# Attention start of a fused kernel: v loaded by unit, the mask and square read from PSUM, one transpose copy moved to ScalarE

## The chip, the cores and the metric

The kernel runs on one core of a Trainium2 chip. The metric is device time of one execution in microseconds, the median of three runs. Times inside the execution come from a profile of one run, counted from the first instruction.

## The reference

Two stages follow each other. The first is an attention with a squared ReLU in place of the softmax, for 8 batches, 12 heads, 448 tokens and a head size of 64. The second is a dense layer with the same activation, on all 3584 tokens.

```python
scores = q @ k.T / sqrt(64)                       # per batch and head, 448 x 448
attn   = max(scores, 0) ** 2 / 448
x      = attn @ v                                  # heads side by side: 3584 x 768
h      = x @ w_in                                  # 3584 x 2048
out    = max(h, 0) ** 2 @ w_out                    # 3584 x 768
```

## The kernel before: the parts concerned

Four heads make a unit, three units make a batch, and the 24 units are numbered n. A unit takes seven rounds, each with 64 keys of every head. A round has four steps: scores on TensorE into a PSUM tile (two such tiles exist), squared ReLU into a tile "at" of fp16, and, three rounds later, the product with v. The rounds are counted from 0 (r = 7n + t). TensorE's order is fixed by the program text; the orders of VectorE, ScalarE and GpSimd are set by the scheduler.

```python
s_p   = tile_pool(name="sps", bufs=2, space=PSUM)     # score tiles, two banks each
mm_p  = tile_pool(name="mmps", bufs=4, space=PSUM)
rel_p = tile_pool(name="widep", bufs=5)               # fp32 tiles in SBUF
at_p  = tile_pool(name="atp", bufs=14)

def load_v(b, parts):                                 # four loads for a batch, each with all three units
    ...
    for i in parts:
        r, e, h = ((0, 0, 0), (1, 0, 2), (0, 1, 3), (1, 1, 1))[i]
        nc.gpsimd.dma_start(out=vst[b][64 * r:64 * r + 64, :, e, :], in_=src[h])

def relu2(ps, dst, scale):                            # L148, L149
    nc.scalar.activation(out=dst, in_=ps, func=AF.Square, scale=scale)
    nc.vector.scalar_tensor_tensor(
        out=dst, in0=ps, scalar=0.0, in1=dst, op0=ALU.is_gt, op1=ALU.mult)

def relu2_wide(ps, dst, scale, eng):                  # L155, L156
    r = rel_p.tile([P, 2, S], FP32, name="rel", tag="wide")
    nc.scalar.activation(out=r, in_=ps, func=AF.Relu, scale=scale)
    eng.tensor_mul(dst, r, r)

def soft(n, t, sp):
    at = at_p.tile([P, 2, S], FP16, name="at", tag="at")
    if n < NPE:                                       # NPE = 6: the first 42 rounds
        relu2_wide(sp[:, :, 0:S], at, SK, nc.gpsimd if n and t == 4 else nc.vector)
    else:
        relu2(sp[:, :, 0:S], at, SK)

def turn_pe(n, w, op):                                # transposes of k and q for units 0 to 5
    ps = mm_p.tile([P, TJ * P], FP16, name="tps", tag="mm")
    for t in range(TJ):
        nc.tensor.transpose(ps[:, t * P:(t + 1) * P], src[:, t, :], ident)
    op(t.rearrange("p t c -> p (t c)"), ps)           # L103, the copy out of PSUM

# the first 23 rounds: attention alone
for r in range(STREAM):                               # STREAM = 23, LAG = 3
    sp = scores(n, t)
    soft(n, t, sp)
    for z in late.get(r, (r - LAG,) if LAG <= r else ()):
        av(*divmod(z, TJ))                            # TensorE: product with v of an earlier round
    ...                                               # loads, casts, transposes of later units

# then two rounds a step, the products with v of a whole unit in one burst,
# and a share of the queued dense matmuls (hps, later ops)
for i in range(STREAM // 2, NB):
    ...
```

From unit 6 on, k and q are transposed by DMA and `relu2` is used throughout.

Of the kernel before, what the change touches and what calls it, by code (L numbers as in the profile page):

```python
# [16 lines left out]
def kernel(  # L17
# [9 lines left out]
    nc = tc.nc  # L27

    B, H, S, D = q.shape
# [7 lines left out]
    TJ = S // TP  # L37
    NU = 3
# [5 lines left out]
    SK = 256.0  # L44
# [29 lines left out]
    def load_qk(n, w, eng):  # L74
        b, u = divmod(n, NU)
        t = raw_p.tile([P, 2, TJ * D], FP32, name=w + "f", tag=w + "f")
        src = q if w == "q" else k
        eng.dma_start(
            out=t,
            in_=src[b, 4 * u:4 * u + 4].rearrange(  # L80
                "(f e) (p t) d -> (e p) f (t d)", e=2, t=TJ))
        raw[n, w] = t

    def cast_qk(n, w, op):
        src = raw.pop((n, w))
        t = blk_p.tile([P, TJ, 2 * D], FP16, name=w + "s", tag=w + "s")
        op(t.rearrange("p t (f d) -> p f t d", f=2),  # L87
           src.rearrange("p f (t d) -> p f t d", d=D))
        blk[n, w] = t

    def turn_dma(n, w):
        t = qkt_p.tile([P, TJ, P], FP16, name=w + "T", tag=w + "T")
        nc.sync.dma_start_transpose(
            out=t, in_=blk.pop((n, w)).rearrange("p t c -> p (t c)"))
        qkt[n, w] = t

    def turn_pe(n, w, op):
        src = blk.pop((n, w))
# [3 lines that stand above are left out]
        t = qkt_p.tile([P, TJ, P], FP16, name=w + "T", tag=w + "T")  # L102
        op(t.rearrange("p t c -> p (t c)"), ps)  # L103
        qkt[n, w] = t

    def load_v(b, parts):
        if b not in vst:
            vst[b] = v_p.tile([P, NU, 2, TJ * D], FP16, name="vs", tag="vs")
        src = v[b].rearrange("(u x) (p t) d -> x p u (t d)", x=4, t=TJ)
        for i in parts:  # L110
            r, e, h = ((0, 0, 0), (1, 0, 2), (0, 1, 3), (1, 1, 1))[i]
            nc.gpsimd.dma_start(out=vst[b][64 * r:64 * r + 64, :, e, :], in_=src[h])  # L112

    w1 = [const_p.tile([P, NM, 512], FP16, name=f"w1_{i}", tag=f"w1_{i}") for i in range(4)]
    w2 = [const_p.tile([P, 4, DM], FP16, name=f"w2_{i}", tag=f"w2_{i}") for i in range(4)]
# [1 line left out]
    def load_w1(i):  # L117
        nc.gpsimd.dma_start(
            out=w1[i],
            in_=moe_w_in[:, 512 * i:512 * (i + 1)].rearrange("(m p) f -> p m f", p=P))  # L120

    def load_w2(i):
        nc.gpsimd.dma_start(
            out=w2[i],
            in_=moe_w_out[512 * i:512 * (i + 1), :].rearrange("(f p) d -> p f d", p=P))
# [21 lines left out]
    def relu2(ps, dst, scale):  # L147
        nc.scalar.activation(out=dst, in_=ps, func=AF.Square, scale=scale)  # L148
        nc.vector.scalar_tensor_tensor(  # L149
            out=dst, in0=ps, scalar=0.0, in1=dst, op0=ALU.is_gt, op1=ALU.mult)  # L150

    def relu2_wide(ps, dst, scale, eng):

        r = rel_p.tile([P, 2, S], FP32, name="rel", tag="wide")
        nc.scalar.activation(out=r, in_=ps, func=AF.Relu, scale=scale)  # L155
        eng.tensor_mul(dst, r, r)  # L156

    def h_groups(b):
        pr = b // 2
# [89 lines left out]

    def soft(n, t, sp):  # L250
        at = at_p.tile([P, 2, S], FP16, name="at", tag="at")
        if n < NPE:
            relu2_wide(sp[:, :, 0:S], at, SK, nc.gpsimd if n and t == 4 else nc.vector)
        else:
            relu2(sp[:, :, 0:S], at, SK)
        ats[n, t] = at
# [3 lines left out]
    def av(n, t):  # L260

        b, u = divmod(n, NU)
        if n == NU * b and t == 0:
            xts[b] = x_p.tile([P, NM, S], FP16, name="xt", tag="xt")
        vs = vst[b]
        if t == 0:
            avs_open[n] = [mm_p.tile([P, 512], FP32, name="avt", tag="mm") for _ in range(2)]
        ap = avs_open[n]
        at = ats.pop((n, t))
        for e in range(2):  # L270
            for c in range(2):
                f = c ^ e
                r = slice(64 * c, 64 * c + 64)
                nc.tensor.matmul(  # L274
                    ap[f][64 * e:64 * e + 64, 0:S],
                    lhsT=vs[r, u, e, t * D:(t + 1) * D],
                    rhs=at[r, e, :],
                    start=(t == 0), stop=(t == TJ - 1), skip_group_check=True)
        if t < TJ - 1:
            return  # L280
        for f in range(2):
            nc.scalar.activation(
                out=xts[b][:, 2 * u + f, :], in_=ap[f][:, 0:S], func=AF.Copy, scale=CX)

    pool, dve, act = nc.gpsimd.tensor_copy, nc.vector.tensor_copy, nc.scalar.copy
# [3 lines left out]
    NPE = 6  # L289
# [11 lines left out]
    def upkeep(i):  # L301

        for n in range(NU, NUN):
            b, u = divmod(n, NU)
            if i == max(TJ * n // 2, STREAM // 2):
                if 5 < n + 3 < NUN:
                    for w in "kq":
                        load_qk(n + 3, w, nc.sync)
                if n == 3:
                    for z in range(4):  # L310
                        load_w2(z)
                if u == 0 and b < B - 1:
                    load_v(b + 1, range(4))
            if i == (TJ * n + 4) // 2:
                if n + 2 < NUN:
                    for w in "kq":
                        cast_qk(n + 2, w, pool)
                if n + 1 < NPE:
                    for w in "kq":
                        turn_pe(n + 1, w, dve)  # L320
                if NPE <= n + 2 < NUN:
                    for w in "kq":
                        turn_dma(n + 2, w)

    with tc.manual_schedule():
        load_qk(0, "k", nc.sync)
        load_qk(0, "q", nc.scalar)
        for n in (1, 2):
            load_qk(n, "k", nc.sync)
            load_qk(n, "q", nc.sync)  # L330
        idle = const_p.tile([P, 512], FP16, name="idle", tag="idle")
        nc.vector.memset(idle, 0.0)
        ident = const_p.tile([P, P], FP16, name="ident", tag="ident")
        make_identity(nc, ident)
        load_v(0, range(4))

        warm = mm_p.tile([P, 512], FP32, name="warm", tag="mm")
        for _ in range(12):
            nc.tensor.matmul(warm, lhsT=idle[:, 0:P], rhs=idle, start=True, stop=True)
        cast_qk(0, "k", dve)  # L340
        cast_qk(0, "q", act)
        turn_pe(0, "k", dve)
        turn_pe(0, "q", dve)
        for w in "kq":
            cast_qk(1, w, pool)
        load_w1(0)

        beside = {
            1: [(load_w1, 1)],
            2: [(cast_qk, 2, "k", pool), (cast_qk, 2, "q", pool),  # L350
                (load_qk, 3, "k", nc.sync), (load_qk, 3, "q", nc.sync)],
            3: [(turn_pe, 1, "k", dve), (load_w1, 2)],
            5: [(turn_pe, 1, "q", dve), (load_w1, 3)],
            7: [(turn_pe, 2, "k", dve)],
            8: [(turn_pe, 2, "q", dve), (load_v, 1, (0, 1))],
            9: [(cast_qk, 3, "k", pool), (cast_qk, 3, "q", pool),
                (load_qk, 4, "k", nc.sync), (load_qk, 4, "q", nc.sync)],
            10: [(load_v, 1, (2, 3))],
            14: [(turn_pe, 3, "k", dve)],
            15: [(turn_pe, 3, "q", dve)],  # L360
            16: [(cast_qk, 4, "k", pool), (cast_qk, 4, "q", pool),
                 (load_qk, 5, "k", nc.sync), (load_qk, 5, "q", nc.sync)],
        }
        late = {21: (18, 19), 22: (20,)}
        for r in range(STREAM):
            n, t = divmod(r, TJ)
# [3 lines that stand above are left out]
                av(*divmod(z, TJ))  # L370
            for fn, *a in beside.get(r, ()):
                fn(*a)
# [3 lines left out]
    for i in range(STREAM // 2, NB):  # L376
        g = []
        for r in range(max(STREAM, 2 * i), 2 * i + 2):
            n, t = divmod(r, TJ)
            g.append((n, t, scores(n, t)))  # L380
        if i in avs:
            for t in range(TJ):
                av(avs[i], t)
        for a in g:
            soft(*a)
        if i in pushes:
            push_dense(pushes[i])
        upkeep(i)
        nxt = min([j for j in pushes if j > i] or [NB + 2])
        run_some(max(0.0, (queued - KEEP) / (nxt - i)))  # L390
# [40 lines left out]
```

## Time and profile before

| what | value |
|---|---|
| device time, median of three | 422.73 us |
| span in the profile | 419.6 us |
| TensorE busy | 395.6 us (94%) |
| VectorE busy | 259.2 us (62%) |
| ScalarE busy | 257.0 us (61%) |
| GpSimd busy | 85.8 us (20%) |
| L156, VectorE, at<-rel | 37 times, mean 1300 ns |
| L149, VectorE, at<-sp,at | 126 times, mean 1086 ns |
| L103, VectorE, kT and qT out of PSUM | 6 times each, 0.61 to 0.62 us |
| first product with v | starts at 10.22 us, its last matmul waits for v until 13.88 us |

The shares are means over the whole span; the kernel has a start of some 80 us, in which attention runs alone or with little dense work, and a long rest in which TensorE has dense work at all times. A row of groups names the line, the engine, the operation, what is written and read, the count, and the mean length of one.

### The profile page before, as it was taken

The numbers are of one execution on the slowest core, as the hardware profiler recorded it, in microseconds if no ns is written. First come the engines' busy times: TensorE is split into PE (matmuls) and PEld (weight loads), VectorE is DVE, ScalarE is ACT, GpSimd is POOL, SyncE is SP. The second block draws the span as 40 slices with busy tenths as digits, with TensorE's granted clock in tenths as the row PEclk, the third lists the DMA queues.
The fourth block names the chain that finished last, engine by engine and source line by source line (L and its number), as shares of the span: only waits on it lengthen the run. The fifth ranks groups of instructions, "written<-read, shape, count | busy, mean of one in ns | idle before, by whom it ended". The sixth has DMA issues, their size and how long they took to land.

```text
span 419.6 us, 7567 instructions
## 1 busy us (share of the span) xinstructions
PE 395.6 (94%) x3104; PEld 199.1 (47%) x3104; DVE 259.2 (62%) x305; ACT 257.0 (61%) x402; POOL 85.8 (20%) x97
## 2 busy tenths in 40 slices
PE   6677968899999999999999999999999999999995
PEld 2232433455455555454455555455455555555562
DVE  3899699885766566686767556677766653223100
ACT  4477869676767666777766565767766564333211
POOL 5973842610141010410141100311000000000000
PEclk9676999999999999999999999999999999999999
DMA  8999999794685643966474655957400111111132
GB/s 253 305 278 244 208 192 209 210 111 121 103 155 154 150 103 98 156 153 137 112 148 137 169 83 126 156 125 159 93 20 21 37 39 39 38 40 37 37 77 75
DMA packets 62883, 53.58 MB, mean 128 GB/s; under 512 B 35712, under 2 KB 59264, under 8 KB 62848
## 3 DMA queue, kind: packets, MB, share of 16 engines
q1 hardware_dynamic: 50672, 40.84, 41.1%
q0 software_dynamic: 11904, 11.80, 17.9%
q8 instruction: 24, 0.39, 0.4%
q10 hardware_dynamic: 272, 0.46, 0.3%
q14 instruction: 11, 0.09, 0.1%
HBM read 45.61 MB, written 11.01 MB: 135 GB/s over the span
## 4 chain that ended last, share of the span: by engine, by line
PE 85%; DVE 8%; DMA 2%; ACT 2%; issue 2%; POOL 1%; POOLq 0%; ACTq 0%
PE ops L198 35%; PE hps L170 34%; PE sp L244 8%; PE avt L274 7%; DVE at L156 6%; DMA vs<-in_v_dram 2%; ACT rel L155 1%; DVE qT L103 1%; POOL vs L112 0%; PE tps L101 0%; DVE kT L103 0%; DVE g L149 0%; DVE at L149 0%; ACT g L148 0%; ACT osb L205 0%
## 5 line engine op out<-in xcount | busy, mean ns | idle before, releaser
L149 DVE SCALAR_TENSOR_TENSOR at<-sp,at 128x896 f16<-128x896 f32 x126 | 131.6, 1086 | 66.0 <-ACT at L148 65.9
L148 ACT ACTIVATE at<-sp 128x896 f16<-128x896 f32 x126 | 108.8, 915 | 40.9 <-PE sp L244 40.5
L198 PEld LDWEIGHTS <-g 128*128 128x128 f16 x896 | 85.3, 98 | 66.6 <-issue 10.3
L149 DVE SCALAR_TENSOR_TENSOR g<-hps,g 128x448 f16<-128x448 f32 x128 | 77.6, 620 | 57.0 <-ACT g L148 56.3
L148 ACT ACTIVATE g<-hps 128x448 f16<-128x448 f32 x128 | 69.6, 550 | 36.0 <-PE hps L170 35.3
L205 ACT ACTIVATE osb<-ops 128x384 f32<-128x384 f32 x56 | 27.6, 494 | 59.5 <-PE ops L198 52.8
L87 POOL CAST ks<-kf 128x896 f16<-128x896 f32 x23 | 23.9, 1040 | 185.9 <-DMA kf<-in_k_dram 165.1
L244 PE MATMUL sp<-qT,kT 64*64 64x448 f16 x672 | 53.8, 376 | 6.6 <-DVE at L149 2.6
L274 PE MATMUL avt<-at,vs 64*64 64x448 f16 x672 | 43.7, 365 | 10.2 <-DVE at L156 3.6
L156 DVE TENSOR_TENSOR at<-rel 128x896 f16<-128x896 f32 x37 | 46.6, 1300 | 4.0 <-ACT rel L155 4.0
L198 PE MATMUL ops<-w_2_96,g 128*128 128x384 f16 x224 | 46.9, 326 | 0.0
L155 ACT ACTIVATE rel<-sp 128x896 f32<-128x896 f32 x42 | 36.9, 924 | 15.6 <-PE sp L244 13.1
L198 PE MATMUL ops<-w_0_94,g 128*128 128x384 f16 x224 | 46.4, 326 | 0.0
L198 PE MATMUL ops<-w_3_97,g 128*128 128x384 f16 x224 | 46.3, 326 | 0.0
L198 PE MATMUL ops<-w_1_95,g 128*128 128x384 f16 x224 | 46.1, 326 | 0.0
L170 PE MATMUL hps<-xt,w_1_91 128*128 128x448 f16 x192 | 41.0, 353 | 1.2 <-DVE g L149 1.2
L170 PE MATMUL hps<-xt,w_2_92 128*128 128x448 f16 x192 | 40.9, 353 | 0.0
L170 PE MATMUL hps<-xt,w_0_90 128*128 128x448 f16 x192 | 40.8, 359 | 0.0
L170 PE MATMUL hps<-xt,w_3_93 128*128 128x448 f16 x192 | 40.5, 353 | 0.0
L274 PEld LDWEIGHTS <-vs 64*64 64x64 f16 x672 | 22.4, 109 | 26.9 <-issue 13.3
L244 PEld LDWEIGHTS <-kT 64*64 64x64 f16 x672 | 15.0, 106 | 36.6 <-issue 32.3
L170 PEld LDWEIGHTS <-w_1_91 128*128 128x128 f16 x192 | 18.1, 98 | 20.0 <-issue 5.0
(33 smaller groups left out, 172.0 us busy)
## 6 DMA issues: line engine op xcount, KB each, us to landing
kf<-in_k_dram SPq DMA_DIRECT2D x24, 448.0 KB, 5.1
out_dram<-osb SPq DMA_DIRECT2D x56, 192.0 KB, 2.7
qf<-in_q_dram SPq DMA_DIRECT2D x23, 448.0 KB, 5.8
vs<-in_v_dram POOLq DMA_DIRECT2D x32, 168.0 KB, 5.2
w_0_90<-in_moe_w_in_dram POOLq DMA_DIRECT2D x1, 768.0 KB, 12.3
w_1_91<-in_moe_w_in_dram POOLq DMA_DIRECT2D x1, 768.0 KB, 20.2
w_2_92<-in_moe_w_in_dram POOLq DMA_DIRECT2D x1, 768.0 KB, 23.6
w_3_93<-in_moe_w_in_dram POOLq DMA_DIRECT2D x1, 768.0 KB, 26.9
```

The lines of the kernel that those rows point to most:

```text
L87: op(t.rearrange("p t (f d) -> p f t d", f=2), src.rearrange("p f (t d) -> p f t d", d=D))
L103: op(t.rearrange("p t c -> p (t c)"), ps)
L148: nc.scalar.activation(out=dst, in_=ps, func=AF.Square, scale=scale)
L149: nc.vector.scalar_tensor_tensor(out=dst, in0=ps, scalar=0.0, in1=dst, op0=ALU.is_gt, op1=ALU.mult)
L155: nc.scalar.activation(out=r, in_=ps, func=AF.Relu, scale=scale)
L156: eng.tensor_mul(dst, r, r)
L170: nc.tensor.matmul(cell[0][:, 0:S], lhsT=w1[f // 4][:, m, (f % 4) * P:(f % 4 + 1) * P], rhs=xt[:, m, :], start=(m == 0), stop=(m == NM - 1))
L198: nc.tensor.matmul(cell[0][:, 0:HALF], lhsT=gt[f][:, tb * P:(tb + 1) * P], rhs=w2[f // 4][:, f % 4, hf * HALF:(hf + 1) * HALF], start=(f = ...
L205: nc.scalar.activation(out=cell[1][:, hf * HALF:(hf + 1) * HALF], in_=cell[0][:, 0:HALF], func=AF.Copy, scale=CO)
L244: nc.tensor.matmul(sp[64 * c:64 * c + 64, e, 0:S].rearrange("p (t c) -> p t c", t=TJ), lhsT=kT[r, t, 64 * e:64 * e + 64], rhs=qT[r, :, 64 ...
L274: nc.tensor.matmul(ap[f][64 * e:64 * e + 64, 0:S], lhsT=vs[r, u, e, t * D:(t + 1) * D], rhs=at[r, e, :], start=(t == 0), stop=(t == TJ - 1 ...
```

## The change

It has three parts. For batches 0 and 1, v comes unit by unit, two loads for a unit with two heads each, so that unit 0 is there before units 1 and 2; the layout of the v tile is turned accordingly (index `e ^ c` in the product). For the first 42 rounds, the square is no longer made by VectorE or GpSimd from an fp32 ReLU in SBUF: ScalarE squares straight from PSUM, and VectorE multiplies that with the mask "score above zero", read from PSUM, as in the rest of the kernel. Five rounds (t = 4 of units 1 to 5) stay on GpSimd in the old form. And of the two copies of transposed k and q, that of q goes to ScalarE for units 1 to 5. The purpose is less work on VectorE in the start and an earlier first product with v.

```diff
-    def load_v(b, parts):
+    def load_v(b, us):
...
-        src = v[b].rearrange("(u x) (p t) d -> x p u (t d)", x=4, t=TJ)
-        for i in parts:
-            r, e, h = ((0, 0, 0), (1, 0, 2), (0, 1, 3), (1, 1, 1))[i]
-            nc.gpsimd.dma_start(out=vst[b][64 * r:64 * r + 64, :, e, :], in_=src[h])
+        src = v[b].rearrange("(u x) (p t) d -> p u x (t d)", x=4, t=TJ)
+        for r in range(2):
+            rows = slice(64 * r, 64 * r + 64)
+            hs = slice(1, 3) if r else slice(0, 4, 3)
+            if isinstance(us, int):
+                nc.gpsimd.dma_start(out=vst[b][rows, us], in_=src[:, us, hs])
+            else:
+                for i, h in enumerate(range(4)[hs]):
+                    nc.gpsimd.dma_start(out=vst[b][rows, :, i], in_=src[:, :, h])
...
-    def relu2_wide(ps, dst, scale, eng):
+    def relu2_pool(ps, dst, scale):
         r = rel_p.tile([P, 2, S], FP32, name="rel", tag="wide")
         nc.scalar.activation(out=r, in_=ps, func=AF.Relu, scale=scale)
-        eng.tensor_mul(dst, r, r)
+        nc.gpsimd.tensor_mul(dst, r, r)
...
-        if n < NPE:
-            relu2_wide(sp[:, :, 0:S], at, SK, nc.gpsimd if n and t == 4 else nc.vector)
+        if 0 < n < NPE and t == 4:
+            relu2_pool(sp[:, :, 0:S], at, SK)
         else:
             relu2(sp[:, :, 0:S], at, SK)
...
-                    lhsT=vs[r, u, e, t * D:(t + 1) * D],
+                    lhsT=vs[r, u, e ^ c, t * D:(t + 1) * D],
...
-                    for w in "kq":
-                        turn_pe(n + 1, w, dve)
+                    turn_pe(n + 1, "k", dve)
+                    turn_pe(n + 1, "q", act)
...
-        load_v(0, range(4))
+        for u in range(NU):
+            load_v(0, u)
...
-            5: [(turn_pe, 1, "q", dve), (load_w1, 3)],
+            5: [(turn_pe, 1, "q", act), (load_w1, 3)],
             7: [(turn_pe, 2, "k", dve)],
-            8: [(turn_pe, 2, "q", dve), (load_v, 1, (0, 1))],
+            8: [(turn_pe, 2, "q", act), (load_v, 1, 0)],
...
-            10: [(load_v, 1, (2, 3))],
+            10: [(load_v, 1, 1)],
+            12: [(load_v, 1, 2)],
             14: [(turn_pe, 3, "k", dve)],
-            15: [(turn_pe, 3, "q", dve)],
+            15: [(turn_pe, 3, "q", act)],
```

More of the change, by code (lines that the diff above doesn't have):

```diff
@@ L312, in upkeep @@
                 if u == 0 and b < B - 1:
-                    load_v(b + 1, range(4))
+                    load_v(b + 1, slice(None))
             if i == (TJ * n + 4) // 2:
```

## The prediction

> **What bounds the kernel now.** I read the page first: its table of slices, its chain, its groups. TensorE is busy 94% of the span, and its digit is 9 from the ninth slice on. The chain says the same by line.
>
> ```profile
> PE 85%; DVE 8%; DMA 2%; ACT 2%; issue 2%; POOL 1%; POOLq 0%; ACTq 0%
> PE ops L198 35%; PE hps L170 34%; PE sp L244 8%; PE avt L274 7%; DVE at L156 6%; DMA vs<-in_v_dram 2%; ACT rel L155 1%; DVE qT L103 1%; POOL vs L112 0%; PE tps L101 0%; DVE kT L103 0%; DVE g L149 0%; DVE at L149 0%; ACT g L148 0%; ACT osb L205 0%
> ```
>
> Of everything that the change touches, only three entries stand in it: the VectorE squares (L156), the load of v, and the transpose copies (L103). To see when they count, I asked for busy time by ten-microsecond stretches (columns: length, busy time and count of TensorE, its weight loads, VectorE, ScalarE, GpSimd; then granted clock, DMA share, GB/s).
>
> ```profile
> 10.00:20.00 10.00, 6.28 (x54) 2.56 (x53) 8.42 (x9) 4.15 (x6) 9.74 (x11) 0.66 1.13 306
> 20.00:30.00 10.00, 7.48 (x89) 3.35 (x85) 9.76 (x9) 7.84 (x10) 7.22 (x6) 0.80 1.14 277
> 30.00:40.00 10.00, 7.14 (x71) 2.74 (x64) 9.57 (x10) 6.86 (x9) 5.32 (x5) 0.67 1.18 258
> 40.00:50.00 10.00, 9.96 (x74) 4.18 (x73) 7.10 (x9) 8.87 (x13) 6.38 (x9) 0.85 1.21 207
> 50.00:60.00 10.00, 6.54 (x73) 3.30 (x72) 9.23 (x10) 6.04 (x10) 5.06 (x5) 1.00 1.17 195
> 80.00:90.00 10.00, 10.00 (x72) 4.77 (x72) 8.06 (x11) 7.73 (x13) 4.36 (x6) 1.00 0.79 109
> ```
>
> From 80 us on TensorE has no gap, so nothing can be won there. All the idle time lies before it: 80 us less the busy 60.9 us of the eight stretches is 19 us. There VectorE is the full engine (9.76 and 9.57 of 10 us), and TensorE runs at a lowered clock. Whatever the start loses or gains passes one to one to the end.
>
> The chain of the first 40 us shows what the start consists of (start, length, what):
>
> ```profile
> 3.46 10.38 DMA vs<-in_v_dram
> 13.88 0.58 PE avt L274
> ...
> 24.47 6.87 DVE at L156 x5
> ```
>
> The first attention product waits for v until 13.88; after that the squares follow one another, five in 6.87 us, or 1.37 us each. The tile view of "at" says that this is not the cost of the work itself (count, then min/median/max in ns):
>
> ```profile
> L156 DVE TENSOR_TENSOR at<-rel x37: 1074/1080/2561, 9.1 to 71.4; 128x896 f16<-128x896 f32 x37
> L149 DVE SCALAR_TENSOR_TENSOR at<-sp,at x10: 1075/1081/1092, 72.9 to 89.9; 128x896 f16<-128x896 f32 x10
> ```
>
> The median square costs 1080 ns but the mean, by the groups, is 1300: some are held up. The form that replaces it, already used after 72 us, costs the same 1081 ns and never above 1092.
>
> **What the Trainium skill says.** "SBUF — State Buffer", section "Who interferes with whom": a VectorE instruction with two SBUF inputs contends with a GpSimd instruction that reads SBUF, one with at most one SBUF input outside the two-port modes does not. The trace agrees: the old square reads the same SBUF tile twice and stretches to 2561 ns while GpSimd is casting; the new one reads PSUM and SBUF and did not stretch beside a GpSimd multiply at 73.20 us. "VectorE: DVE Perf Modes", "The perf-mode tier table": a two-tensor operation on fp32, or with PSUM, runs at the lowest rate; hence no difference in the plain cost, as both rows show. "TensorE: Matmul & The Clock Gate", "What's actually happening": the clock falls to half after an idle window of about 3.4 us and returns after a busy one. The trace shows 0.54 for 12 to 16 us, right behind the 3.7 us that TensorE waited for v. "Perfetto Trace Analysis", "DMA Optimizations": splitting a transfer may let some of the work start sooner; here DMA is already full, and the gain is only in the order of arrival.
>
> **The change, part by part.**
>
> (1) v of batch 0. Four loads of all three units become six loads of one unit each, unit 0 first; bytes are the same. Half of v had landed by 10.22 us in the old order, the rest at 11.87 and 13.88. A third of v, coming first, should then be there before 10 us, when it is first needed. The issue costs GpSimd two more loads at 0.63 us, in time in which it waits for k anyway (2.85 us idle before its first cast). Wait removed: the 3.6 us between 10.22 and 13.88. But the next limit is near. The fifth scores started at 15.25 us. In the new program their PSUM buffer is free only after the third VectorE operation. Starting from the first scores at 7.69: ScalarE ends at 9.04, VectorE at 10.15 and 11.19; the third and fourth scores start there, VectorE ends with the third at 12.65, and the fifth scores start at 12.7. Gain so far: 2.55 us.
>
> (2) The squares. All 37 on VectorE go from 1300 to 1081 ns: 37 x 0.22 = 8.1 us of VectorE time, and GpSimd's casts, which stretched to 1.6 to 1.8 us against 0.94 alone, get faster too. But the PSUM tile is no longer released by ScalarE; VectorE now holds it. There are two such tiles. The later part of the old trace runs exactly this loop once without other work (start, length, engine, what, and the releaser in brackets):
>
> ```profile
> 74.03 0.38 PE L244 MATMUL sp<-qT,kT 64*64 64x448 f16 x4 [1.98 <-DVE at L149]
> ...
> 74.46 1.92 ACT L148 ACTIVATE at<-sp 128x896 f16<-128x896 f32 x2 [1.60 <-PE sp L244]
> ...
> 75.43 1.07 DVE L149 SCALAR_TENSOR_TENSOR at<-sp,at 128x896 f16<-128x896 f32 x1
> ```
>
> From 74.03: 0.38 + 0.05 + 0.92 + 0.05 + 1.08 + 0.04 = 2.5 us until the buffer is free. Two buffers make 1.25 us a round, against 1.37 in the old square-bound stretch. So the engine that was the bound is relieved by 0.22 us a round and the wait that takes its place gives back most of it. At the lowered clock, four scores take 0.59 us and the loop 2.7.
>
> (3) The copies. Five qT copies leave VectorE (5 x 0.615 = 3.1 us) for ScalarE, where an operation of 896 columns takes 0.92: 4.6 us. ScalarE then has, in seven rounds, 7 x 0.82 (its pitch back to back), one copy 0.82 and two attention copies 0.97: 7.5 us. It is not the bound, but it stands in the same loop: a copy ahead of a square delays a tile that VectorE and TensorE wait for.
>
> Following rounds 4 to 23 with these lengths in the order in which the changed program lists its instructions, each scores group starting when the tile two rounds before is free, I get the 25th scores at 40.5 us; before they began at 43.37. That is a gain of 2.9 us at the full clock, of about 1 us if the clock is lowered in half of the rounds as now (10 rounds x 0.1, and 1 us on seven dense matmuls).
>
> (4) Rounds 24 to 43, mixed with the first dense work. Before, ScalarE could run ahead through five buffers; TensorE needed 30.66 us (43.37 to 74.03). In the changed order, VectorE takes squares 26 to 29 after the third dense group, whose last matmul comes after scores 26 and 27; ScalarE has that order too. So scores 28 wait till that group is evacuated: they start 3.9 us after scores 26, with 1.9 us of TensorE work between. Later pairs wait 0.7 to 1.5 us for the second buffer in most steps. Adding up the ten steps, I get 32.4 us: a loss of 1.7.
>
> Sum: start 2.9 (or 1) less 1.7, so +1.2 us at best, -0.7 with a lowered clock. The copies of later v, the dense stage and the stores are untouched. I allow 1 us more because the first lowering of the clock followed the removed wait, and take 1.2 us: 421.5.
>
> **The rivals.** A: VectorE time is what counts, because it was full to 40 us. Then 8.1 + 3.1 = 11.2 us less VectorE work would show almost whole, capped by the 19 us of idle TensorE: some 412 us. For it: 9.76 of 10 us busy; against it: the two-tile loop, which I find at 1.25 us a round. B: the longer hold of PSUM and ScalarE's copies cost more than I see, every step of the mixed stage waiting for both tiles: three more steps like that of scores 28, at 1.5 us each, make 426. For it: the old kernel was able to buffer five rounds, and the new one two. C: the start is bound by DMA (share 1.1 to 1.2 up to 80 us), so earlier squares only wait for k and q. Against it: in the old trace GpSimd's long waits for k lie after 62 us and their tiles are needed ten microseconds later. It would give 422.
>
> **Range and chances.** My balance is a small difference of two sums of 2 to 3 us, each with an error of 1.5 us or so, and the clock adds 1. That gives 417.5 to 425 for 8 in 10. Faster by over 2% needs under 414.3 us, which only rival A brings: 0.07. Slower by over 2% needs over 431.2, three times the loss of rival B: 0.02. Within 2%: 0.91.
>
> **What would show it.** Right: no wait for v before the first attention product; VectorE's squares at 1.08 us in the first 40 us and idle between them, waiting for ScalarE; scores waiting for VectorE in total 8 us or more; scores 25 before 42.5 us and scores 45 within 2 us of 74. Wrong: VectorE still full to 40 us, or a TensorE without gaps from 45 us on, which would be rival A; v arriving after 11.6 us, which would take step 1 away.

## The result and the profile after

The changed kernel takes 424.47 us (median of 4 runs, 424.28 to 425.32); the kernel before, run beside it, 422.58 us. The ratio is 1.006, with a 95% interval of 1.003 to 1.0089: a small loss where a small gain had been forecast, though inside the forecast range of 417.5 to 425. Ratios leave out executions more than 1.5% above the fastest of their kernel, so a ratio need not be the quotient of the two medians given with it.

The size of the loss is less sure than this interval says. In four later series the kernel before has medians from 422.83 to 423.61 us (137 executions in all), which leaves a loss of 0.9 to 1.6 us. The profiled spans are 422.5 us after and 419.6 before, but the profiled execution of before (421.42 us) lies 1.4 to 2.2 us below these medians, while that of the changed kernel (424.32 us) lies at its own. So that much of the 2.9 us between the spans belongs to the choice of execution and not to the change.

The page of the changed kernel, its chain by engine and by line, and two of its groups (count, then busy time and mean ns of one, then the idle time ahead of them and what ended it):

```profile
PE 86%; ACT 3%; SPq 3%; DVE 2%; POOL 2%; issue 2%; DMA 1%; POOLq 0%
PE ops L204 35%; PE hps L176 33%; PE sp L250 9%; PE avt L280 6%; SPq L93 2%; ACT at L154 2%; DVE at L155 2%; DMA qf<-in_q_dram 1%; PE warm L346 1%; PE tps L101 1%; POOL at L162 1%; POOL qs L87 1%; POOL ks L87 1%; SPq L78 0%; ACT rel L161 0%
...
L155 DVE SCALAR_TENSOR_TENSOR at<-sp,at 128x896 f16<-128x896 f32 x163 | 170.8, 1087 | 79.8 <-ACT at L154 79.0
...
L250 PE MATMUL sp<-qT,kT 64*64 64x448 f16 x672 | 54.7, 380 | 19.4 <-DVE at L155 16.8
```

The same row of scores in the kernel before:

```profile
L244 PE MATMUL sp<-qT,kT 64*64 64x448 f16 x672 | 53.8, 376 | 6.6 <-DVE at L149 2.6
```

The load of v is no longer in the chain, and the share of VectorE fell from 8% to 2%. In its place stand the squares on ScalarE (L154), VectorE's masks, and GpSimd with SyncE's queue (SPq): multiplies (L162), casts of q and k (L87), and the loads and transposes of q and k that SyncE issues. The rows of scores show the exchange: TensorE is now idle 19.4 us ahead of scores, 16.8 of them for the VectorE operation that releases a PSUM tile; before it was 6.6 us, 2.6 of them for that operation. In return it is idle 1.8 us ahead of products with v, where it was 10.2.

The stretches of the start, after (columns as in the prediction):

```profile
10.00:20.00 10.00, 8.38 (x84) 3.88 (x87) 8.52 (x10) 7.00 (x8) 8.71 (x13) 0.66 1.14 295
20.00:30.00 10.00, 6.46 (x65) 2.72 (x64) 6.57 (x8) 7.34 (x11) 2.91 (x4) 0.63 1.14 278
30.00:40.00 10.00, 6.28 (x67) 3.20 (x67) 6.55 (x7) 8.01 (x11) 4.90 (x5) 0.67 1.18 250
...
```

VectorE came down from 9.76 and 9.57 us of ten to 6.57 and 6.55, and that bought nothing: TensorE is less busy from 20 to 40 us than before. Its granted clock is no higher, 0.66, 0.63 and 0.67 against 0.66, 0.80 and 0.67.

The whole effect lies in the start. The table cuts it at the starts of the scores of certain rounds in the two traces (round n is that of the (n+1)th group of four score matmuls). The stretch from round 46 to the end is 339.6 us in both kernels.

| stretch, us | before | after | after less before | forecast |
|---|---|---|---|---|
| start to round 4 | 15.25 | 12.81 | -2.44 | -2.55 |
| round 4 to 24 | 28.12 | 30.64 | +2.52 | -0.3 (full clock) |
| round 24 to 44 | 30.66 | 31.49 | +0.83 | +1.7 |
| round 44 to 46 | 5.96 | 7.97 | +2.01 | nothing |
| sum | 79.99 | 82.91 | +2.92 | -1.2 |

So the load of v does gain 2.4 us, and that is gone 20 rounds later. Two of the four stretches need a cause.

**Rounds 4 to 24.** The chain of the changed kernel, 13.8 to 20.9 us (start, length, what; a product with v is left out at the dots, and pieces of 0.05 us or less):

```profile
13.81 0.59 PE sp L250 x4
...
14.77 0.87 PE tps L101 x7
15.66 0.91 ACT qT L103
16.57 0.83 ACT at L154
17.42 1.10 DVE at L155
18.57 0.61 PE sp L250 x4
19.20 0.92 ACT at L154
20.12 0.80 ACT qT L103
20.92 0.83 ACT at L154
```

Scores, square, mask, scores: the loop over two PSUM tiles is the path, and the two copies of transposed q on ScalarE are inserted in it. In rounds 4 to 24 TensorE is idle for 7.9 us; 6.3 us of that end with a mask, 1.5 us with a ReLU of ScalarE, and none with a load. Before, it was idle for 6.2 us. The rest of the difference is TensorE's own work, 22.7 us at a mean clock of 0.62 against 21.9 us at 0.69. How long one turn takes is seen undisturbed later on (TensorE's timeline of the changed kernel; start, length, what, and in brackets the idle time ahead and its releaser):

```profile
37.69 0.59 PE L250 MATMUL sp<-qT,kT 64*64 64x448 f16 x4 [1.57 <-DVE at L155]
...
40.42 0.59 PE L250 MATMUL sp<-qT,kT 64*64 64x448 f16 x4 [0.65 <-DVE at L155]
40.94 2.58 PE L176 MATMUL hps<-xt,w_0_90 128*128 128x448 f16 x7
```

40.42 - 37.69 = 2.73 us for two rounds. The four scores take 0.59 us, and seven dense matmuls 2.58 us where a group of seven at 44.75 us takes 1.49: the granted clock is lowered here, 0.60 in the stretch from 40 to 44 us against 1.00 in the next.

**Rounds 44 to 46.** GpSimd's timeline of the changed kernel:

```profile
75.12 0.93 POOL L87 CAST ks<-kf 128x896 f16<-128x896 f32 x1 [3.04 <-DMA kf<-in_k_dram]
76.27 0.93 POOL L87 CAST qs<-qf 128x896 f16<-128x896 f32 x1 [0.21 <-DMA qf<-in_q_dram]
77.16 1.68 POOL L162 TENSOR_TENSOR at<-rel 128x896 f16<-128x896 f32 x1
```

and TensorE's of the same kernel:

```profile
78.89 0.76 PE L280 MATMUL avt<-at,vs 64*64 64x448 f16 x12 [1.83 <-POOL at L162]
```

The multiply of round 39 stands in GpSimd's order behind two casts that wait for their loads. Its input, ScalarE's ReLU, had started at 67.26 us and takes 0.91. The product with v then stands 1.83 us. In the kernel before, the scheduler had put the same multiply ahead of these two casts:

```profile
73.20 1.68 POOL L156 TENSOR_TENSOR at<-rel 128x896 f16<-128x896 f32 x1
75.86 0.93 POOL L87 CAST ks<-kf 128x896 f16<-128x896 f32 x1 [0.97 <-DMA kf<-in_k_dram]
```

There the product of that unit started without a wait, although the loads of k and q landed no earlier. The change did not touch this multiply; it moved the order around it.

### The profile page after: what moved, and what is told of

It is laid out like the page before. It is cut to its first block, busy times and chain, and to the rows that moved or that the text cites. A ratio compares the mean times of both kernels' runs of the same rounds, so it can differ in the third digit from the quotient of the medians.

```text
span 422.5 us, 7557 instructions
## 1 busy us (share of the span) xinstructions
PE 395.3 (94%) x3104; PEld 200.3 (47%) x3104; DVE 249.9 (59%) x300; ACT 261.9 (62%) x407; POOL 79.9 (19%) x101
## 4 chain that ended last, share of the span: by engine, by line
PE 86%; ACT 3%; SPq 3%; DVE 2%; POOL 2%; issue 2%; DMA 1%; POOLq 0%
PE ops L204 35%; PE hps L176 33%; PE sp L250 9%; PE avt L280 6%; SPq L93 2%; ACT at L154 2%; DVE at L155 2%; DMA qf<-in_q_dram 1%; PE warm L346 1%; PE tps L101 1%; POOL at L162 1%; POOL qs L87 1%; POOL ks L87 1%; SPq L78 0%; ACT rel L161 0%
## 5 line engine op out<-in xcount | busy, mean ns | idle before, releaser
L155 DVE SCALAR_TENSOR_TENSOR at<-sp,at 128x896 f16<-128x896 f32 x163 | 170.8, 1087 | 79.8 <-ACT at L154 79.0
L154 ACT ACTIVATE at<-sp 128x896 f16<-128x896 f32 x163 | 142.1, 917 | 51.1 <-PE sp L250 50.3
L155 DVE SCALAR_TENSOR_TENSOR g<-hps,g 128x448 f16<-128x448 f32 x128 | 77.7, 620 | 59.9 <-ACT g L154 59.3
L154 ACT ACTIVATE g<-hps 128x448 f16<-128x448 f32 x128 | 69.3, 550 | 35.9 <-PE hps L176 35.1
L250 PE MATMUL sp<-qT,kT 64*64 64x448 f16 x672 | 54.7, 380 | 19.4 <-DVE at L155 16.8
L87 POOL CAST ks<-kf 128x896 f16<-128x896 f32 x23 | 21.6, 938 | 188.8 <-DMA kf<-in_k_dram 168.0
L250 PEld LDWEIGHTS <-kT 64*64 64x64 f16 x672 | 16.6, 107 | 53.7 <-issue 50.2
L176 PEld LDWEIGHTS <-w_0_90 128*128 128x128 f16 x192 | 18.3, 99 | 18.9 <-issue 4.2
L280 PEld LDWEIGHTS <-vs 64*64 64x64 f16 x672 | 21.4, 111 | 12.3 <-issue 2.5
L176 PEld LDWEIGHTS <-w_1_91 128*128 128x128 f16 x192 | 18.1, 98 | 18.9 <-issue 3.8
L176 PEld LDWEIGHTS <-w_3_93 128*128 128x128 f16 x192 | 18.0, 98 | 18.9 <-issue 3.9
```

Source lines behind the costliest of these rows:

```text
L87: op(t.rearrange("p t (f d) -> p f t d", f=2), src.rearrange("p f (t d) -> p f t d", d=D))
L155: nc.vector.scalar_tensor_tensor(out=dst, in0=ps, scalar=0.0, in1=dst, op0=ALU.is_gt, op1=ALU.mult)
L176: nc.tensor.matmul(cell[0][:, 0:S], lhsT=w1[f // 4][:, m, (f % 4) * P:(f % 4 + 1) * P], rhs=xt[:, m, :], start=(m == 0), stop=(m == NM - 1))
L250: nc.tensor.matmul(sp[64 * c:64 * c + 64, e, 0:S].rearrange("p (t c) -> p t c", t=TJ), lhsT=kT[r, t, 64 * e:64 * e + 64], rhs=qT[r, :, 64 ...
L280: nc.tensor.matmul(ap[f][64 * e:64 * e + 64, 0:S], lhsT=vs[r, u, e ^ c, t * D:(t + 1) * D], rhs=at[r, e, :], start=(t == 0), stop=(t == TJ ...
```

## The experiments

All times are medians; "before" is the kernel before, run in the same series; intervals are 95%.

**One part at a time: v by unit alone.** The diff is that of the change for `load_v`, its calls and the index of v; squares and copies stay as before.

```diff
-        load_v(0, range(4))
+        for u in range(NU):
+            load_v(0, u)
...
-            8: [(turn_pe, 2, "q", dve), (load_v, 1, (0, 1))],
+            8: [(turn_pe, 2, "q", dve), (load_v, 1, 0)],
...
-            10: [(load_v, 1, (2, 3))],
+            10: [(load_v, 1, 1)],
+            12: [(load_v, 1, 2)],
```

> Part 1 alone: v of batches 0 and 1 by unit, squares and copies as before. Theory (the three parts work on different waits): scores of round 4 start near 12.8 us instead of 15.25, VectorE stays the bound of the start as before, so the 2.4 us are kept to the end: about 420.2 us against 422.6. Rival (the start is limited further on by VectorE or by the arrival of k and q, whatever v does): the gain is eaten up by round 24, scores 24 again near 43.4 us, and the time is 422.6.

Measured: 424.0 us against 423.21, ratio 1.0021 (0.9997 to 1.0045), no clear difference; the rival was nearer. Round 4 starts at 11.08 us, 4.2 us earlier than before, and round 11 at 26.19, 2.8 us later. The timelines of VectorE and GpSimd in this kernel:

```profile
9.13 7.17 DVE L162 TENSOR_TENSOR at<-rel 128x896 f16<-128x896 f32 x4 [1.43 <-ACT rel L161]
...
9.21 1.80 POOL L87 CAST qs<-qf 128x896 f16<-128x896 f32 x1 [1.23 <-DMA qf<-in_q_dram]
```

The first four old squares follow one another, three of them stretched (1.81 to 2.69 us), 1.79 us on average instead of 1.08; two casts of GpSimd in that time take twice their 0.93. Then TensorE stands 3.7 us for a transpose copy behind them:

```profile
20.64 0.59 PE L250 MATMUL sp<-qT,kT 64*64 64x448 f16 x4 [3.70 <-DVE qT L103]
```

This is what "SBUF — State Buffer", section "Who interferes with whom", of the Trainium skill says of a VectorE operation with two SBUF inputs beside GpSimd; the run adds what it costs here. It is not the new order of v that brings the collision: in the run with the copies alone, below, v comes as before, and the first four squares take the same 7.17 us (5.56 in the profiled run of before). The ninth square starts at 23.98 us in both. This points to VectorE's squares as what sets the pace with or without the wait for v; scores that start earlier only wait further on.

**The squares alone**, v and copies as before:

```diff
-        if n < NPE:
-            relu2_wide(sp[:, :, 0:S], at, SK, nc.gpsimd if n and t == 4 else nc.vector)
+        if 0 < n < NPE and t == 4:
+            relu2_wide(sp[:, :, 0:S], at, SK, nc.gpsimd)
```

> Part 2 alone: ScalarE squares from PSUM and VectorE applies the mask from PSUM, v and copies as before. Theory (the hold of the two PSUM tiles till VectorE is done replaces VectorE as the bound): scores 4 still at 15.3 us, scores 24 at 44.5 to 45.5 us, and a GpSimd multiply of round 39 that stands behind a cast of unit 9; 424.5 to 425.5 us. Rival (the copies on ScalarE are what made the change slow): VectorE 4 us less busy in the first 40 us and the time at 420.5 to 422.5.

Measured: 424.83 us against 423.21, ratio 1.0043 (1.0026 to 1.006), slower by less than half a per cent, as the theory had it. Round 4 starts at 15.21 us, as before, and round 24 at 46.53, 3.2 us later than before and a microsecond later than forecast. The scores wait 15.7 us for VectorE in twenty places. The operation is not dearer; the PSUM tile is held longer. Between rounds 4 and 24 TensorE is idle 7.7 us instead of 6.2, and its own work takes 23.6 us at a mean clock of 0.61 instead of 21.9 at 0.69, so that about half of the 3.2 us goes with the clock.

**The copies alone.**

```diff
-            5: [(turn_pe, 1, "q", dve), (load_w1, 3)],
+            5: [(turn_pe, 1, "q", act), (load_w1, 3)],
...
-                    for w in "kq":
-                        turn_pe(n + 1, w, dve)
+                    turn_pe(n + 1, "k", dve)
+                    turn_pe(n + 1, "q", act)
```

> Part 3 alone: the five qT copies on ScalarE, v and squares as before. Theory (VectorE is the bound of the old start, ScalarE has room there and frees the PSUM tile itself): 5 times 0.55 us less on VectorE, 1 to 2.5 us gained, 420 to 421.6 us. Rival (a copy in ScalarE's order holds the scores back): 423.5 to 424.5 us.

Measured: 425.7 us against 423.21, ratio 1.0022 (0.9992 to 1.0052); its 22 runs lie between 421.2 and 428.4. In the profiled run the first four squares take 7.17 us from 9.04 on, 5.56 in that of before, though nothing ahead of them was changed. Inconclusive: the scatter of 7 us is larger than the 1 to 2.5 us that the copies were expected to bring.

**Two parts, without the copies**: the two diffs above of v and of the squares together.

> Parts 1 and 2, without part 3: both copies of k and q on VectorE. Theory (the two PSUM tiles held till VectorE is done, at a lowered clock, set 1.5 us a round; where the q copy runs does not matter): scores 24 at 43 to 44 us, scores 44 at 74.5 to 76, 423.5 to 425 us. Rival (ScalarE's copies in the same loop cost 0.8 us each): scores 24 at 41 to 42 us and 422 us or less.

Measured: 423.46 us against 422.83, ratio 1.0016 (1.0001 to 1.0032). Round 4 starts at 12.77 us (12.81 with the copies on ScalarE), round 24 at 44.09 (43.45), round 44 at 77.17, later than forecast, at a mean clock of 0.91 from round 24 on. The copies are not what takes the gain away; on either engine they stand in the same loop. Here GpSimd's multiply of round 39 stands ahead of the second of the two casts (75.26 us), the product with v does not wait for it, and rounds 44 to 46 take 5.93 us.

**The multiply of round 39 off GpSimd**, in the changed kernel; it becomes square and mask like its neighbours:

```diff
-        if 0 < n < NPE and t == 4:
+        if 0 < n < NPE - 1 and t == 4:
```

> The changed kernel, with the one multiply of round 39 taken from GpSimd and done in the mask form on VectorE. Theory (1.8 us of the loss come from that multiply standing behind the casts of unit 9, which wait for their transfers): no wait of the product with v for GpSimd near 79 us, and 422.4 to 423 us against 424.4. Rival (without it the product waits as long for something else, or the extra VectorE work of 1.1 us costs as much): 424 to 424.5 us.

Measured: 423.97 us against 423.21, ratio 1.0014 (0.9995 to 1.0033). The wait is gone: rounds 44 to 46 take 5.93 us, as before the change. By the ratios (1.006 less 1.0014) that is worth 1.9 us, by the two medians 0.5 us, and the intervals of the two ratios just touch; the time is close to the rival's 424 and not in the theory's range. In the profiled run rounds 24 to 44 took 33.57 us instead of 31.49, which hides it in the span (421.8 us). No new wait does that: TensorE is idle 6.6 us there, 7.0 in the changed kernel, but the same work takes 27.0 us at a mean clock of 0.92 instead of 24.5 at 1.00. So the wait is shown to come from that multiply; that it costs its whole 2.0 us in every run is not.

**The clock.** The changed kernel with two idle matmuls of 512 columns after each round from 4 to 22 that has no transposes; they keep TensorE busy and nobody waits for their output.

```diff
+            if r >= 4 and not any(x[0] is turn_pe for x in beside.get(r, ())):
+                keep = mm_p.tile([P, 512], FP32, name="keep", tag="mm")
+                for _ in range(2):
+                    nc.tensor.matmul(keep, lhsT=idle[:, 0:P], rhs=idle, start=True, stop=True)
```

> The changed kernel, with two idle matmuls of 512 columns (0.43 us) after each of rounds 4 to 22 that has no transposes, results not used. Theory (a part of the loss in the start is TensorE's lowered clock of 0.5 to 0.6 between 12 and 44 us, which its gaps bring about): the clock near 1 from 16 us on, scores 24 at 40 to 41.5 us against 43.45, 421.5 to 422.5 us. Rival (the clock follows, and ScalarE and VectorE set the rounds): scores 24 at 43.5 us or later, 424.4 us or more.

Measured: 425.39 us against 422.83, ratio 1.0054 (1.0033 to 1.0074): the theory's round 24 and the rival's time. Busy time in a stretch of 4 us, first of the changed kernel, where the clock (third number from the end) is low in most stretches of the start:

```profile
28.00:32.00 4.00, 3.98 (x38) 2.09 (x38) 2.91 (x4) 2.85 (x4) 0.54 (x1) 0.50 1.14 280
```

and then with the idle matmuls, where it is 1.00 from 20 to 48 us:

```profile
28.00:32.00 4.00, 3.21 (x40) 1.57 (x40) 3.59 (x4) 3.46 (x5) 0.17 (x1) 1.00 1.14 278
```

Rounds 4 to 24 took 27.92 us (13.44 to 41.36), at a mean clock of 0.94 instead of 0.62; the forecast for the full clock was 27.8, and the changed kernel took 30.64. So some 2.7 us of the second stretch of the table go with the lowered clock, more than the whole loss there. But the gain did not reach the end. Round 44 starts at 74.88 us, as in the changed kernel (74.94). Rounds 24 to 44, first of the changed kernel, then with the idle matmuls:

```profile
43.45:74.94 31.49, 24.53 (x233) 11.46 (x232) 24.16 (x30) 26.41 (x38) 15.16 (x17) 1.00 1.20 223
```

```profile
41.36:74.88 33.52, 26.17 (x234) 11.78 (x234) 25.07 (x31) 26.73 (x38) 15.21 (x18) 0.95 1.20 216
```

Of the 2.0 us lost there, 1.6 are longer matmuls (26.17 against 24.53 us busy) at a lower clock (0.85 from 48 to 52 us, 0.72 from 52 to 56, where the changed kernel has 1.00), and 0.4 are longer waits. "TensorE: Matmul & The Clock Gate", section "HAM oscillation", of the Trainium skill describes idle gaps of more than about 3.4 us that bring the low clock back. That is not what is seen here: in the changed kernel no gap of TensorE from 12.8 to 44 us is over 1.57 us, and the clock was at 0.50 to 0.60 in most of that time. Why the clock falls again at 48 us is not shown by any run.

**GpSimd's queue.** In the changed kernel GpSimd stands 4.62 us at 31.46 us ahead of its sixteenth load, a load of v of batch 1. Here v of batch 1 comes in four loads of all units, as in later batches:

```diff
-            8: [(turn_pe, 2, "q", act), (load_v, 1, 0)],
+            8: [(turn_pe, 2, "q", act), (load_v, 1, slice(None))],
...
-            10: [(load_v, 1, 1)],
-            12: [(load_v, 1, 2)],
```

> The changed kernel, with v of batch 1 in four loads issued at once. Theory (GpSimd's stand for a free load is in the changed kernel too, 4.6 us at 27 to 31 us, but off the path, since nobody waits for what follows): the stand gone, the time as in the changed kernel, 424 to 425 us, but for the multiply of round 39, which the order on GpSimd leaves behind the two casts of unit 9 as before. Rival (the stand delays the casts of unit 4 and so the start): 2 us or more faster, 422.4 us or less.

Measured: 424.64 us against 423.46, ratio 1.0031 (1.0006 to 1.0056). GpSimd no longer stands there, and round 24 starts at 44.28 us (43.45 with the stand). The time is as forecast, and the stand is off the path of the changed kernel.

**The mask only in unit 0.** If the collisions of e1's first squares are all that part 2 has to avoid, seven masks are enough. From v by unit alone:

```diff
-        if n < NPE:
+        if 0 < n < NPE:
             relu2_wide(sp[:, :, 0:S], at, SK, nc.gpsimd if n and t == 4 else nc.vector)
```

> Part 1, with the mask form in unit 0 alone (rounds 0 to 6) and the old squares from unit 1 on. Theory (part 1 alone lost its 4 us because the first four squares, reading SBUF twice, ran beside GpSimd's casts at 1.79 us each): the first squares at 1.08 us, scores 4 at 12.8 us and scores 11 at 22 to 23.5 us against 26.2 of part 1 alone; 420.5 to 422.5 us. Rival (what ate the gain was not the first squares): scores 11 at 25 us or later, 423.5 us or more.

Measured: 426.58 us against 422.83, ratio 1.009 (1.0058 to 1.0121), the slowest of all. Rounds 4 and 11 start at 12.91 and 21.02 us, well ahead of the kernel before, as the theory had it, and round 24 at 42.16, still 1.2 us ahead; the total is the rival's. The old squares of later units meet the casts. VectorE's timeline:

```profile
31.96 8.96 DVE L162 TENSOR_TENSOR at<-rel 128x896 f16<-128x896 f32 x5 [0.49 <-ACT rel L161]
...
50.10 8.91 DVE L162 TENSOR_TENSOR at<-rel 128x896 f16<-128x896 f32 x6
```

That is 1.79 and 1.49 us on average; single squares of the two rows take 4.72 and 3.17 us, beside two casts and a multiply of GpSimd at 32.27 to 35.7 and four casts from 49.63 on. Rounds 24 to 44 take 34.61 us (30.66 before).

**An fp16 ReLU.** The old form let ScalarE release the PSUM tile at once and run five rounds ahead; its weakness was the slow square. So: v by unit, old form, but ScalarE's ReLU is rounded to fp16 in SBUF, and VectorE multiplies fp16 by fp16.

```diff
-        r = rel_p.tile([P, 2, S], FP32, name="rel", tag="wide")
+        r = rel_p.tile([P, 4, S], FP16, name="rel", tag="wide")[:, 0:2, :]
         nc.scalar.activation(out=r, in_=ps, func=AF.Relu, scale=scale)
```

> Part 1, and the old ReLU into SBUF by ScalarE but as fp16, so that VectorE's multiply of the first 42 rounds has 16-bit operands (about 0.55 us if it runs twice as fast) and PSUM is released by ScalarE. Theory (the start needs both: a short hold of PSUM and a short VectorE step): rounds at 1.0 to 1.2 us, scores 24 at 36 to 39 us, scores 44 at 67 to 71, 416 to 420 us. Rival (the start is bound by the arrival of k, q and weights, or by collisions of two-input VectorE operations with GpSimd): scores 24 at 42 us or later and 422 us or more.

Measured: 420.51 us against 422.83, ratio 0.9941 (0.9917 to 0.9965). "VectorE: DVE Perf Modes", section "The perf-mode tier table", of the Trainium skill gives a two-tensor operation on 16-bit (bf16) operands in SBUF twice the rate of fp32. Here, with fp16, one multiply gets 1.73 times as fast (count, min/median/max ns):

```profile
L162 DVE TENSOR_TENSOR at<-rel x37: 608/624/4286, 9.4 to 70.5; 128x896 f16<-128x896 f16 x37
```

624 ns against 1080, with a maximum of 4286 where it meets GpSimd. Round 18 starts at 28.15 us, 6.4 us earlier than before; round 24, at 40.83, and the time both fall between theory and rival. From round 18 on GpSimd, off the path before, is on it. Its timeline, and TensorE's:

```profile
32.00 0.59 POOL L115 DMA_DIRECT2D vs<-in_v_dram  x1 [6.92 <-PE sp L250]
...
34.36 1.68 POOL L162 TENSOR_TENSOR at<-rel 128x896 f16<-128x896 f16 x1
...
36.09 0.96 PE L280 MATMUL avt<-at,vs 64*64 64x448 f16 x8 [4.26 <-POOL at L162]
```

GpSimd stands 6.92 us ahead of its sixteenth load, with the multiply of round 18 behind that load, and the product waits 4.26 us for it. What ends the stand is the landing of its eighth load, a block of w_in, at 31.71 us, and not TensorE's scores, which the brackets name: the loads of GpSimd take eight semaphores in turn, and from the ninth on each waits for the one of the load eight places before it; in the changed kernel and in the kernel before, too, the held-up load starts 0.29 us after that landing (31.46 after 31.17 us, 43.34 after 43.05). The limit is one of this program's semaphores, and no run shows one of the chip.

**The same with v of batch 1 in four loads.**

```diff
-            8: [(turn_pe, 2, "q", dve), (load_v, 1, 0)],
+            8: [(turn_pe, 2, "q", dve), (load_v, 1, slice(None))],
...
-            10: [(load_v, 1, 1)],
-            12: [(load_v, 1, 2)],
```

> The fp16-ReLU kernel, with v of batch 1 in four loads issued at once instead of six. Theory (GpSimd's queue stood 6.9 us at its sixteenth load because only eight of its loads may be under way, so the sixteenth waits for the landing of the eighth, a weight block; the multiply of round 18 behind it held TensorE 4.3 us): the fifteenth load is now the first of w_out, behind that multiply; no GpSimd wait before the multiply, scores 24 at 36 to 38 us against 40.8, and 416 to 419 us. Rival (the start is held by something that this only uncovers): scores 24 earlier, but the last scores of the start (44) at 73 us again and 420.5 us.

Measured: 418.96 us against 423.46, ratio 0.9912 (0.9886 to 0.9939). Round 24 starts at 35.36 us instead of 40.83. The edit that brought nothing in the changed kernel brings 5.5 us here to round 24, since here GpSimd's multiply is waited for. At round 44 2.3 us of that are left (71.04 against 73.34). New waits follow: 3.3 us for v of batch 1, 3.7 us for GpSimd's multiplies in four places, and 2.2 us for q transposed by DMA.

**And without GpSimd's multiplies**, and with the casts of units 5 to 7 on VectorE:

```diff
-            relu2_wide(sp[:, :, 0:S], at, SK, nc.gpsimd if n and t == 4 else nc.vector)
+            relu2_wide(sp[:, :, 0:S], at, SK, nc.vector)
...
-                        cast_qk(n + 2, w, pool)
+                        cast_qk(n + 2, w, dve if n + 2 < 8 else pool)
```

> As the run with four loads, and GpSimd multiplies nothing in the first 42 rounds, and k and q of units 5 to 7 are cast by VectorE: from then on GpSimd has only loads till its casts of unit 8. Theory (VectorE's operations with two SBUF inputs stand behind GpSimd's casts, 7 us for six multiplies near 49 to 56 us): the multiplies near 0.62 us all through after 30 us, scores 24 at 36 to 38 us, scores 44 at 67 to 70 us, 414 to 418 us. Rival (casts in VectorE's order wait for arriving k and q and hold the multiplies back): 419 us or more.

Measured: 416.52 us against 423.46, ratio 0.9852 (0.9815 to 0.9888), as forecast; from 26 us on every multiply takes 0.61 to 0.63 us. Two things were changed at once here, and which of them brings how much is not separated. The largest wait that remains is for v of batch 1; TensorE's timeline:

```profile
44.03 0.37 PE L280 MATMUL avt<-at,vs 64*64 64x448 f16 x1 [1.64 <-DMA vs<-in_v_dram]
49.17 2.83 PE L280 MATMUL avt<-at,vs 64*64 64x448 f16 x27 [4.76 <-DMA vs<-in_v_dram]
```

**And v of batch 1 ahead of the third and fourth block of w_in.**

```diff
-            3: [(turn_pe, 1, "k", dve), (load_w1, 2)],
-            5: [(turn_pe, 1, "q", dve), (load_w1, 3)],
+            3: [(turn_pe, 1, "k", dve), (load_v, 1, slice(None))],
+            5: [(turn_pe, 1, "q", dve), (load_w1, 2)],
             7: [(turn_pe, 2, "k", dve)],
-            8: [(turn_pe, 2, "q", dve), (load_v, 1, slice(None))],
+            8: [(turn_pe, 2, "q", dve), (load_w1, 3)],
```

> The previous version with one change of order: the four loads of v of batch 1 are issued two places earlier, ahead of w_in blocks 2 and 3. Theory (the attention product of unit 3 stands 1.64 and 4.76 us for v of batch 1 because that v is queued behind w_in blocks 2 and 3, and nothing else would hold TensorE then): both waits for v between 42 and 49 us go, scores 44 start 3 us or more before 69.5 us, and the time falls from 416.5 to 410 to 413.5 us. Rival (the DMA share is full to 80 us, so whatever is moved back arrives later and holds TensorE in its turn: w_in blocks 2 and 3, or k and q of units 6 and 7): a new DMA wait of 3 us or more appears before 80 us, and the time stays at 415.5 us or more.

Measured: 413.07 us against 423.61 (411.25 to 413.82 in 4 runs), ratio 0.9746 (0.9702 to 0.979). Both waits for v are gone, and round 44 starts at 66.27 us, 3.2 us earlier than in the version just before (69.48). The rival is right in part: a new wait of a DMA appears. TensorE's timeline:

```profile
63.02 0.96 PE L250 MATMUL sp<-qT,kT 64*64 64x448 f16 x8 [4.20 <-DMA qT<-qs]
```

q of unit 6 is the first that a DMA transposes; it was issued at 42.64 us and landed 20 us later, with the DMA engines full. About half of what was moved forward is paid back there; the rest is kept. This is the fastest kernel of the study, 2.5% below the kernel before, and the only one that clears 2%. Its span less the start of round 46 (412.0 less 72.41) is 339.6 us, so here too the whole gain lies in the start.

## Why the prediction was wrong

**What held.** Step 1: no wait for v remains, and the fifth scores start at 12.81 us (forecast 12.7). Step 2: every mask of the start takes 1080 to 1092 ns, VectorE falls to two thirds busy, and scores wait for it 16.8 us, twice the "8 us or more". Rival A, in which VectorE's time counts, did not come: there are no 412 us, though VectorE was freed by 3 us in ten. In step 4, scores 28 start 4.0 us after scores 26 (50.16 less 46.16; forecast 3.9), and the ten steps cost 0.83 us more than before where 1.7 had been said: the mechanism right, the size half.

**What failed.** Two terms. First, the clock. In "that is a gain of 2.9 us at the full clock, of about 1 us if the clock is lowered in half of the rounds as now", the sum for the full clock held up (27.8 us forecast, 27.92 in the run with idle matmuls, at a mean clock of 0.94). The term for the clock was mis-sized: 1.9 us was set against it, and it measured 2.8 (30.64 less 27.8), because the clock was at 0.50 to 0.60 in six of the eight 4 us stretches from 12 to 44 us, not in half of them. Waits of 0.6 to 1.6 us in eight of the twenty rounds went with a clock that did not stay up. So round 24 starts at 43.45 us, where 43.37 was before and 42.5 the limit named.

The forecast then took the better branch. With the lowered clock the sum was -0.7, and with the 1 us allowed it makes 0.3; the 1.2 us taken is the sum at the full clock. And "I allow 1 us more because the first lowering of the clock followed the removed wait" had no ground: with that wait gone, the stretch from 12 to 16 us shows 0.56, before it was 0.54. Nor was the wait for v one idle stretch of 3.7 us: that is a sum over weight loads, while the matmuls stood for v twice, 1.28 and 1.64 us.

Second, "the copies of later v, the dense stage and the stores are untouched" left out that GpSimd's order would be made anew. The multiply of round 39 slid behind casts that wait for their loads and held TensorE 1.83 us. This was in the order of the changed kernel's instructions, but whether it hurts depends on when k and q land. It is 2.0 of the 2.9 us by which the spans differ; the rest, 0.9 us, is the start and the mixed stage together (-2.44 + 2.52 + 0.83). Its size over all runs stays open, since taking the multiply away moved the median by 0.5 us and the ratio by 0.0046.

That those 0.9 us lie so near the -0.7 of the branch with the lowered clock is luck: by round 24 the start came out 1.1 us worse than that branch, and the mixed stage 0.9 us better.

Two readings were off without deciding anything. The five squares that the chain has in 6.87 us (1.37 each) take 8.03 us on VectorE's timeline from 24.40 us on, 1.61 each, so the old bound was slower there than the prediction took it to be. And ScalarE's ReLU (L155, 1%), which the change also replaces, stands in the chain too.

Rival B (426 us, a longer hold of PSUM in every mixed step) comes nearest by its number and is not what happened: the mixed stage lost even less than the sum of step 4. Rival C (422 us, squares that only wait for k and q) fails in the traces: up to round 46 no idle stretch of TensorE ends with the landing of k or q, before or after; in the changed kernel they reach it only through GpSimd's multiply.

**Why each part alone brings nothing.** In the old form VectorE's squares seem to set the pace, stretched where they meet GpSimd's casts, whether v is early or late. The mask form is not stretched, and pays with the two-tile loop. Together they bring 2.4 us by round 4 and lose 2.5 us by round 24. The version that wins keeps the long run-ahead of the old form and makes its VectorE operation shorter (624 ns), then takes GpSimd's multiplies and the order of loads out of the way. That the number of PSUM tiles is what makes the loop so long was not tried by giving it a third tile.

## What to carry to other kernels

Before moving work off a full engine, ask which buffer the new form holds and for how long: a PSUM tile that two engines must read, with two tiles in all, sets a loop of 2.5 to 2.7 us for two rounds here, though from 20 to 40 us no engine was busy for more than 8.01 us of ten. Making the held-up operation cheaper (here fp16 in SBUF, 624 against 1080 ns) can bring more than moving it. On an engine that takes its work in order, look at what stands ahead of the one operation that somebody waits for: casts and loads that wait for a DMA pass their wait on.

## What the runs showed of the hardware that was not expected

- TensorE's clock was at 0.50 to 0.60 in six of the eight 4 us stretches from 12 to 44 us without any gap over 1.57 us from 12.8 us on, with TensorE 74% busy (23.6 of 32 us); two further matmuls of 512 columns a round brought it to 1.00 (from 20 us on).
- VectorE's two-input operations beside GpSimd stretched from 1.08 to 1.79 us on average over four (fp32), a single one to 4.72 us, and single fp16 ones from 0.62 to 4.29 us. The mask, which reads PSUM and SBUF, stayed at 1.08 to 1.09 us in all its executions up to round 46.
- Executions of one kernel differ with the granted clock: of the 75 executions of the kernel before in one series, the fifteen from 421.15 to 421.47 us have a mean granted clock of 0.976 over the span, and the fifteen from 423.89 to 427.44 us 0.969. Which is cause and which is consequence is not shown by this.
- A cast of 896 columns from fp32 to fp16 takes 0.62 us on VectorE and 0.93 on GpSimd.
